# Two linear-attention and squared-ReLU layers on one core: the attention work beside the dense stages written out turn by turn in a fixed engine order, and GpSimd's part of it given to VectorE

## The chip, the core and the metric

The kernel runs on one core of a Trainium2 chip. The engines of that core are named as the profile names them: PE (TensorE, matmuls; PEld is its weight load), DVE (VectorE), ACT (ScalarE), POOL (GpSimd) and SP (SyncE, whose instruction queue here issues the DMA transfers). PSUM is the memory that matmuls write, SBUF the one that all engines read. Each engine works through its own list of instructions in the order of that list; semaphores hold an instruction until its inputs are there. The metric is the device time of one execution in microseconds (us).

## The reference, cut to what matters

Two layers, each an attention block and a dense block with a residual add, on a sequence of S = 2048 rows of D = 576 features, H = 32 heads of 18, and F = 4608 hidden features; the weights of both layers are the same arrays.

```python
def A(x):                                   # x is layernorm(x) of the stream
    q, k, v = split(x @ wqkv)               # 32 heads of 18
    pq, pk  = q @ w_phi, k @ w_phi          # per head
    phi_q = concat(softmax(pq), softmax(-pq))
    phi_k = concat(softmax(pk), softmax(-pk))
    kv, z = phi_k^T v, sum over rows of phi_k      # sums over the whole sequence
    o = (phi_q @ kv) / (phi_q . z + 1e-6)
    return o @ wo
def B(x):
    h = relu(x @ w1 + b1)
    return (h * h) @ w2 + b2
x = x + A(layernorm(x)); x = x + B(layernorm(x))   # twice
```

## The kernel before

**Tiling.** The rows are worked in four blocks of 512 (`TB`), each of four tiles of 128 (`NT`); the hidden features in 36 tiles of 128 (`NF`). Every fp32 operand is held as a high and a low part, and each product is made of three matmuls (high by high, high by low, low by high). Since `kv` and `z` are sums over the whole sequence, a layer's queries can be finished only when the keys of all four blocks are in. So the kernel runs block after block through the dense part (`g_mlp`), and beside the dense part of one block it does the attention work of others: the queries, the output projection and the norm of the block whose dense stage comes next, and, in layer 1, also the norm, keys and values (for layer 2) of the block whose dense stage has just ended.

**A dense stage.** It takes 36 turns, one for a feature tile `f`: `first(f + 1)` brings the weights of the next tile, `hidden(f)` (L703) is 14 matmuls of 512 columns into one PSUM bank called `h`, `square(f)` evacuates that bank on ACT (L709 ReLU with bias, L710 square) and splits the result on DVE (L713 cast to the high part, L714 low part, tile `hb`), and `second(f - 1)` (L729 and L721, 15 matmuls) multiplies the previous tile's result with `w2` into the accumulators `acc`. So `hidden(f + 1)` waits until the ReLU has emptied `h`, and `second(f)` waits for `hb`. In the first dense stage of the whole program the weights are raw fp32: a tile `rr` is loaded (L679, L166, L681; two buffers), copied on ACT into the high part (L682 for `w1`, L684 for `w2`), subtracted on DVE for the low part (L683, L685, and 128 columns of `w2` on POOL at L686), and stored back to DRAM (tile `dw`, L687 and L688). The seven later stages load these parts.

**The attention work.** For each row tile: project (L377) and copy to SBUF (L397); `soft` takes the maximum and minimum of each head (L414, L415), subtracts on DVE (L418, one half of 576 columns) and on POOL (L419, the other half), takes the exponential on ACT (L420) and the sums on DVE (L423). For queries, `g_phi` multiplies with the key sums `zb` (L572 on DVE, L573 on POOL, reduction L574), and scales (L590, one half on each of the two). For keys, POOL does the scaling alone (L431). `g_out` transposes the features (L610), splits them (L611, L612), multiplies with `kv` (L624, L626, L628), projects with `wo` (L646, L649), adds `b2` on POOL (L653), and `g_norm` normalizes and transposes (L321, L335, L336, L337).

**What sets the order.** The attention work is a generator, `g_back`, woven into the turns: one step of it is written behind each turn (a step and a half in layer 1 from the second stage on). That is only the order in which instructions are written; a list scheduler with a cost model then puts each engine's instructions into the order that it deems best, so on ACT and DVE the attention's instructions stand where the scheduler put them. In the stage that follows a bridge, a further rule (`issue_after`) keeps the softmax work behind the last `L714` written.

**The stages of the program**, by the trace (us from the start of the span):

| stage | from | to | dense block | beside it |
|---|---|---|---|---|
| D0 | 266.6 | 543.1 | m_3, raw weights | softmax, output and norm of block 2 |
| D1 | 543.1 | 861.0 | m_2 | norm, values, keys of block 3 for layer 2; queries to norm of block 0 |
| D2 | 861.0 | 1179.3 | m_0 | the same for blocks 2 and 1 |
| D3 | 1179.3 | 1429.0 | m_1 | norm and keys of block 0 for layer 2 |
| bridge | 1429.0 | 1559.3 | none | last keys, sums, queries of two blocks |
| D4 | 1559.3 | 1828.5 | m_1 | softmax, output and norm of the next block |
| D5 | 1828.5 | 2112.2 | m_0 | queries to norm of the next block |
| D6 | 2112.2 | 2395.4 | m_3 | queries to norm of the last block |
| D7 | 2395.4 | 2626.6 | m_2 | nothing |

The names in the trace carry the block (`m_2ph` is the bank `h` of the dense stage of block 2, `a_0Q3e` the exponentials of the fourth query tile of block 0), and the two layers' stages of one block share a name.

## Time and profile before

| | us |
|---|---|
| median of three runs | 2634.07 |
| lowest and highest | 2630.38, 2634.8 |
| the profiled execution: its own time | 2632.79 |
| the profiled execution: span of the trace | 2631.1 |
| granted PE clock, mean over the span | 0.988 |

The span is what the profiler shows of one execution, from the first to the last instruction; 1.7 us of that execution's own time lie around it. The page gives for each engine its busy time and share of the span. A matmul that waits is idle time of PE, and the list of waits gives that idle time by the instruction that ended it. The granted clock tells at which share of full speed PE ran: a busy PE at clock 0.50 does half the work. A row of the timeline reads: start, duration, engine, line, operation, output and inputs, shapes, and in brackets the idle time of that engine before it and what ended it.

### The profile page before, as it was taken

How to read it: one execution, taken by the hardware profiler on the slowest of the kernel's cores; microseconds unless marked ns; L12 is line 12 of the kernel's file. 1: busy time of each engine (PE TensorE's matmuls, PEld its weight loads, DVE VectorE, ACT ScalarE, POOL GpSimd, SP SyncE). 2: the span in 40 equal slices, each digit the busy share in tenths (PEclk: the TensorE clock that was granted, in tenths of full speed). 3: DMA queues.
4: the chain of work that ended last, by engine and by line, in shares of the span. 5: the costliest groups of instructions: out<-in, count | busy, mean ns of one | idle time of the engine just before them, and what ended most of it. 6: DMA issues, size and time to landing. Idle time of an engine off the chain costs nothing.

```text
span 2631.1 us, 37728 instructions
## 1 busy us (share of the span) xinstructions
PE 2548.2 (97%) x15396; PEld 2236.5 (85%) x15396; DVE 1107.3 (42%) x1866; ACT 712.6 (27%) x1180; POOL 380.1 (14%) x425
## 2 busy tenths in 40 slices
PE   8998899999999999999999999999999999999999
PEld 7897688888888888888888987888888888888887
DVE  6777844343623346344212675222622262222111
ACT  3333343422221222313222332212222122212221
POOL 3441411112201022012000222010200030010000
PEclk9998999999999999999999999999999999999999
DMA  8513677885655766556666245556755575556665
GB/s 310 159 55 110 236 261 251 280 299 209 214 169 176 279 209 208 161 202 205 214 198 199 87 154 177 170 181 232 237 181 171 189 235 190 169 182 215 195 199 169
DMA packets 163615, 522.02 MB, mean 198 GB/s; under 512 B 21659, under 2 KB 51003, under 8 KB 161395
## 3 DMA queue, kind: packets, MB, share of 16 engines
q1 hardware_dynamic: 163443, 519.61, 59.7%
q8 instruction: 122, 2.00, 0.3%
q14 instruction: 50, 0.41, 0.0%
HBM read 434.91 MB, written 84.64 MB: 197 GB/s over the span
## 4 chain that ended last, share of the span: by engine, by line
PE 83%; DVE 9%; POOL 2%; DMA 2%; issue 2%; ACT 1%; SPq 0%; DVEq 0%; POOLq 0%; ACTq 0%
PE m_2ph L703 8%; PE m_0ph L703 8%; PE m_1ph L703 8%; PE m_3ph L703 7%; PE m_2acc L729 6%; PE m_1acc L729 6%; PE m_0acc L729 6%; PE m_3acc L729 6%; PE m_2acc L721 2%; PE m_1acc L721 2%; PE m_0acc L721 2%; PE m_3acc L721 2%; PE a_2po L646 1%; PE a_0po L646 1%; PE v_2pv L377 1%
## 5 line engine op out<-in xcount | busy, mean ns | idle before, releaser
L703 PE MATMUL m_0ph<-a_0nh,m_0h 128*128 128x512 f32 (+1 forms) x760 | 230.3, 386 | 7.8 <-ACT m_0hr L709 7.6
L703 PE MATMUL m_2ph<-a_2nh,m_2h 128*128 128x512 f32 (+1 forms) x760 | 228.5, 384 | 3.0 <-ACT m_2hr L709 3.0
L729 PE MATMUL m_3acc<-m_3s,m_3hb 128*128 128x448 f32 x864 | 194.4, 369 | 6.7 <-DVE m_3hb L714 5.1
L729 PE MATMUL m_1acc<-m_1s,m_1hb 128*128 128x448 f32 x864 | 191.9, 369 | 4.7 <-DVE m_1hb L714 2.8
L729 PE MATMUL m_0acc<-m_0s,m_0hb 128*128 128x448 f32 x864 | 190.6, 367 | 1.8 <-DVE m_0hb L713 1.5
L729 PE MATMUL m_2acc<-m_2s,m_2hb 128*128 128x448 f32 x864 | 190.0, 367 | 1.8 <-DVE m_2hb L713 1.5
L729 PEld LDWEIGHTS m_3acc<-m_3s,m_3hb 128*128 128x128 f32 x864 | 161.3, 188 | 28.1 <-DVE m_3hb L714 7.4
L729 PEld LDWEIGHTS m_1acc<-m_1s,m_1hb 128*128 128x128 f32 x864 | 161.9, 189 | 24.8 <-DVE m_1hb L714 4.5
L729 PEld LDWEIGHTS m_2acc<-m_2s,m_2hb 128*128 128x128 f32 x864 | 161.6, 188 | 20.2 <-DVE m_2hb L713 2.0
L729 PEld LDWEIGHTS m_0acc<-m_0s,m_0hb 128*128 128x128 f32 x864 | 161.5, 188 | 20.1 <-DVE m_0hb L713 2.0
L703 PEld LDWEIGHTS m_0ph<-a_0nh,m_0h 128*128 128x128 f32 x760 | 141.2, 190 | 37.6 <-ACT m_0hr L709 8.4
L703 PEld LDWEIGHTS m_2ph<-a_2nh,m_2h 128*128 128x128 f32 x760 | 140.3, 189 | 32.4 <-ACT m_2hr L709 3.4
L713 DVE CAST m_2hb<-m_2hr 128x512 fp32r<-128x512 f32 x72 | 31.7, 440 | 293.1 <-ACT m_2hr L710 293.1
L713 DVE CAST m_1hb<-m_1hr 128x512 fp32r<-128x512 f32 x72 | 32.2, 447 | 268.7 <-ACT m_1hr L710 268.6
L713 DVE CAST m_0hb<-m_0hr 128x512 fp32r<-128x512 f32 x72 | 33.6, 467 | 235.0 <-ACT m_0hr L710 235.0
L709 ACT ACTIVATE m_1hr<-m_1ph,b1t 128x512 f32<-128x512 f32 x72 | 49.4, 686 | 305.5 <-PE m_1ph L703 298.4
L709 ACT ACTIVATE m_2hr<-m_2ph,b1t 128x512 f32<-128x512 f32 x72 | 49.4, 686 | 299.4 <-PE m_2ph L703 285.2
L709 ACT ACTIVATE m_0hr<-m_0ph,b1t 128x512 f32<-128x512 f32 x72 | 49.4, 686 | 273.7 <-PE m_0ph L703 259.5
L703 PE MATMUL m_3ph<-a_3nh,m_3h 128*128 128x512 f32 (+1 forms) x380 | 114.7, 385 | 4.6 <-ACT m_3hr L709 4.6
L703 PE MATMUL m_0ph<-a_0nl,m_0h 128*128 128x512 f32 (+1 forms) x304 | 117.3, 386 | 0.0
L703 PE MATMUL m_3ph<-t0onh,m_3h 128*128 128x512 f32 (+1 forms) x380 | 114.4, 385 | 2.9 <-ACT m_3hr L709 2.5
L703 PE MATMUL m_2ph<-a_2nl,m_2h 128*128 128x512 f32 (+1 forms) x304 | 116.6, 384 | 0.0
(1379 smaller groups left out, 5684.5 us busy)
## 6 DMA issues: line engine op xcount, KB each, us to landing
m_2h<-dw SPq DMA_DIRECT2D x72, 640.0 KB
m_0h<-dw SPq DMA_DIRECT2D x72, 640.0 KB
m_1h<-dw SPq DMA_DIRECT2D x72, 640.0 KB
m_2s<-dw SPq DMA_DIRECT2D x72, 576.0 KB
m_0s<-dw SPq DMA_DIRECT2D x72, 576.0 KB
m_1s<-dw SPq DMA_DIRECT2D x72, 576.0 KB
dw<-m_3h SPq DMA_DIRECT2D x36, 640.0 KB
m_3h<-dw SPq DMA_DIRECT2D x36, 640.0 KB
```

The costliest lines, as they stand in the source:

```text
L377: nc.tensor.matmul(pt[:, :HP], a, m, start=(k == 0), stop=(k == 3 * KC + 1))
L646: nc.tensor.matmul(pt[:, :HP], a, m[:w, g], start=(g == 0 and k == 0), stop=(g == NG - 1 and k == 2))
L703: nc.tensor.matmul(ph[:, cols], a, m, start=(k == 0), stop=(k == 3 * KC + 1))
L709: nc.scalar.activation(hr, ph, AF.Relu, bias=b1t[:, f : f + 1])
L713: nc.vector.tensor_copy(hh, hr)
L721: nc.tensor.matmul(acc[KC], a, m, start=(f == 0 and k == 0), stop=(f == NF - 1 and k == 2))
L729: nc.tensor.matmul(acc[t][:, :R], a[:, rows], m, start=(f == 0 and k == 0), stop=(f == NF - 1 and k == 2))
```

## The change

The change writes the attention work of all eight dense stages as a table of turns, and has PE, ACT, DVE and POOL keep the order in which the instructions are written (`manual_schedule`); SP's transfers, and all that lies outside the dense stages, are still put in order by the scheduler. A turn now has two places where attention work can stand: behind `square(f)`, and behind `second(f - 1)`. `Plan.put(turn, depth, ...)` means the second of them (or, for half turns, the first of the turn after); within a place, deeper (older) work stands first. Each query tile takes three turns: maxima and subtractions in the first, the exponential, the sums and the product with `zb` in the second, the scaling in the third. Everything of the attention that POOL did is now on DVE (L467 for L419, a single 1152-wide multiply L741 for L572 and L573 and L478 for L590 and for L431, L701 for L653, and the whole low part of `w2` at L817); POOL keeps two small operations of each norm. In the dense loop, `first` is cut in two: `first` (the `w1` part) stays ahead of `hidden(f)`, `first2` (the `w2` part) stands behind `second(f - 1)`, and `second(0)` stands behind the first two places of a stage. Attention outputs are transposed and multiplied two a turn instead of one, and the turns of the norm come behind the last projection. The output weights are loaded in the first turns of the queries' work, the query weights and the spilled normalized rows two turns ahead of them. The loop variable `n` is used anew, so that the dense tiles of five stages are called `m3...` in the changed kernel.

```diff
+    class Plan:
+        def put(self, turn, depth, call, *args):
+            slot = round(2 * turn) + 1
+            entries = self.at.setdefault(slot, [])
+            entries.append((-depth, len(entries), call, args))
+        def slots(self):
+            for slot in range(max(self.at, default=-1) + 1):
+                for _, _, call, args in sorted(self.at.get(slot, ()), key=lambda e: e[:2]):
+                    call(*args)
+                yield
...
+    def exponents(raw, name):
...
+        nc.vector.tensor_reduce(mm[:, 0], v, op=ALU.max, axis=AX.X)
+        nc.vector.tensor_reduce(mm[:, 1], v, op=ALU.min, axis=AX.X)
+        nc.vector.tensor_sub(e4[:, 0], v, m[:, 0])
+        nc.vector.tensor_sub(e4[:, 1], m[:, 1], v)
+        return e
+    def totals(e, r):
+        nc.scalar.activation(e, e, AF.Exp)
+        nc.vector.tensor_reduce(r, e.rearrange("p s (h d) -> p s h d", d=DH), op=ALU.add, axis=AX.X)
+        nc.vector.reciprocal(r, r)
+    def scaled(e, r):
...
+        nc.vector.tensor_mul(e3, e3, r2.unsqueeze(2).to_broadcast([P, 2 * H, DH]))
...
-            nc.gpsimd.tensor_add(x, x, b2t)
+            nc.vector.tensor_add(x, x, b2t)
...
+    def plan_queries(plan, at, gap, layer, raws, er, ph, name):
...
+        for t in range(NT):
+            plan.put(at + gap * t, 0, first, t)        # exponents
+            plan.put(at + gap * t + 1, 1, second, t)   # totals, product with zb, its sums
+            plan.put(at + gap * t + 2, 2, third, t)    # scaled
+        return at + gap * (NT - 1) + 2
+    def plan_attend(plan, at, gap, layer, b, raws, dst, name, otags, queries=None):
...
+        if queries:
+            for t in range(NT):
+                plan.put(at + gap * t, 0, queries, t)
+            at += 1
+        for n, call in enumerate(calls):               # loads of the output weights
+            plan.put(at + n, 9, call)
+        at = plan_queries(plan, at, gap, layer, raws, [], out.ph, name) + 1
+        for i in range(2 * NG):
+            plan.put(at + i / 2, 0, out.turn, i)
+            plan.put(at + (i + 1) / 2, 1, out.times, i)
+        at += NG + 1
+        for t in range(NT):
+            plan.put(at + t - 1, 9, out.load, t)
+        plan_norm(plan, Norm(dst, f"{name}n", out.keep), out.project, [at + t for t in range(NT)],
+                  [at + 1, at + 2, at + 4, at + 5], [at + 4 + t for t in range(NT)], [at + 5, at + 7])
...
         def first(f):
...
                 nc.scalar.activation(h1, r1, AF.Copy)
                 nc.vector.tensor_sub(l1, r1, h1.bitcast(F32))
+                nc.sync.dma_start(dense1[f], both1)
...
+        def first2(f):
+            h1, l1, r2, ph = parts[f]
...
             if fresh:
                 nc.scalar.activation(s2[:, :D], r2, AF.Copy)
-                nc.vector.tensor_sub(s2[:, D : D + R], r2[:, :R], s2[:, :R].bitcast(F32))
-                nc.gpsimd.tensor_sub(s2[:, D + R : 2 * D], r2[:, R:], s2[:, R:D].bitcast(F32))
+                nc.vector.tensor_sub(s2[:, D : 2 * D], r2, s2[:, :D].bitcast(F32))
...
         for f in range(2):
             hidden(f, halves[1])
             square(f)
-        second(0)
         yield
         yield
+        second(0)
         first(2)
+        first2(2)
+        yield
+        yield
         for f in range(2, NF):
             if f + 1 < NF:
                 first(f + 1)
             hidden(f, every)
             square(f)
+            yield
             second(f - 1)
+            if f + 1 < NF:
+                first2(f + 1)
             yield
...
+                plan_norm(plan, Norm(xk, f"n{m}"), lambda t, done=done: done[t],
+                          (0, 0, 1, 2), (1, 1, 2, 3), (2, 3, 4, 5), (3, 5))
...
+                    plan.put(4 + t, 0, keys, t)
+                    if i < NB - 1:
+                        plan.put(4 + t, 0, values, t)
+                    plan.put(5 + t, 1, soft1, t)       # exponents of the keys
+                    plan.put(6 + t, 2, soft2, t)       # totals, scaled
+                    if i < NB - 1:
+                        plan.put(7 + t, 3, add, t)
...
+                at = 10
+            if i + 1 < NB:
+                if i == 0:
+                    plan_attend(plan, 0, 3, layer, nb, nxt_raws, nxt, n2, TAGS_C if layer else TAGS_A)
+                else:
...
+                    start = at - 2 if at else 0
+                    for n, call in enumerate(calls):   # loads of the query weights
+                        plan.put(start + n / 4, -2, call)
+                    plan.put(start, -3, lambda held=held, nb=nb, n2=n2: held.update(unspill(nb, f"{n2}u")))
+                    plan_attend(plan, at or 3, 2, layer, nb, raws2, nxt, n2, TAGS_C,
+                                lambda t, held=held, qw=qw, raws2=raws2, n2=n2:
+                                raws2.append(make_raw(held, t, qw, f"{n2}q")))
...
-            weave(g_mlp(layer, b, ready, rows, f"m{n}", layer == 0 and i == 0), g_back(),
-                  1.0 if layer or i == 0 else 1.5)
+            with tc.manual_schedule(engines=ordered):
+                weave(g_mlp(layer, b, ready, rows, f"m{n}", layer == 0 and i == 0), plan.slots(), 1.0)
```

ACT's list in D1, around the last two query tiles of block 0, before the change (`hr` is the dense turn's evacuated tile, `ph` the bank `h`, `a_0Q3e` the exponentials of the last query tile):

```order
L420 ACTIVATE a_0Q2e<-a_0Q2e 128x1152
L709 ACTIVATE m_2hr_7081<-m_2ph_6993,b1t 128x512
L710 ACTIVATE m_2hr_7081<-m_2hr_7081 128x512
L397 ACTIVATE a_0qs_7102<-a_0qp_7103 128x288
L397 ACTIVATE a_0qs_7102<-a_0qp_7119 128x288
L420 ACTIVATE a_0Q3e<-a_0Q3e 128x1152
L709 ACTIVATE m_2hr_7168<-m_2ph_7066,b1t 128x512
L710 ACTIVATE m_2hr_7168<-m_2hr_7168 128x512
```

And the same place in the changed kernel:

```order
L471 ACTIVATE a_0Q2e<-a_0Q2e 128x1152
L420 ACTIVATE a_0qs_7175<-a_0qp_7176 128x288
L420 ACTIVATE a_0qs_7175<-a_0qp_7192 128x288
L837 ACTIVATE m3hr_7225<-m3ph_7130,b1t 128x512
L838 ACTIVATE m3hr_7225<-m3hr_7225 128x512
L837 ACTIVATE m3hr_7276<-m3ph_7210,b1t 128x512
L838 ACTIVATE m3hr_7276<-m3hr_7276 128x512
L471 ACTIVATE a_0Q3e<-a_0Q3e 128x1152
L837 ACTIVATE m3hr_7323<-m3ph_7261,b1t 128x512
L838 ACTIVATE m3hr_7323<-m3hr_7323 128x512
```

Between the copy of the last query tile (L420 now, L397 before) and its exponential there was no other work, so the exponential stood ahead of the next ReLU; now two turns' evacuations stand between them.

DVE's list at the start of D0 before the change (`m_3h_2` and `m_3s_2` are the parts of `w1` and `w2` of tile 2, `hb` the split result, `a_2Q0` the first query tile):

```order
L683 TENSOR_TENSOR m_3h_2_3597<-m_3rr_3599,m_3h_2_3597 128x640
L713 CAST m_3hb_3534<-m_3hr_3531 128x512
L714 TENSOR_TENSOR m_3hb_3534<-m_3hr_3531,m_3hb_3534 128x512
L683 TENSOR_TENSOR m_3h_3_3612<-m_3rr_3614,m_3h_3_3612 128x640
L713 CAST m_3hb_3554<-m_3hr_3551 128x512
L714 TENSOR_TENSOR m_3hb_3554<-m_3hr_3551,m_3hb_3554 128x512
L414 TENSOR_REDUCE a_2Q0m<-t0q2qs_2913 128x32
L415 TENSOR_REDUCE a_2Q0m<-t0q2qs_2913 128x32
L418 TENSOR_TENSOR a_2Q0e<-t0q2qs_2913,a_2Q0m 128x576
```

And in the changed kernel:

```order
L841 CAST m_3hb_3534<-m_3hr_3531 128x512
L842 TENSOR_TENSOR m_3hb_3534<-m_3hr_3531,m_3hb_3534 128x512
L841 CAST m_3hb_3554<-m_3hr_3551 128x512
L842 TENSOR_TENSOR m_3hb_3554<-m_3hr_3551,m_3hb_3554 128x512
L464 TENSOR_REDUCE a_2Q0m<-t0q2qs_2913 128x32
L465 TENSOR_REDUCE a_2Q0m<-t0q2qs_2913 128x32
L466 TENSOR_TENSOR a_2Q0e<-t0q2qs_2913,a_2Q0m 128x576
L467 TENSOR_TENSOR a_2Q0e<-a_2Q0m,t0q2qs_2913 128x576
L804 TENSOR_TENSOR m_3h_2_3583<-m_3rr_3584,m_3h_2_3583 128x640
L817 TENSOR_TENSOR m_3s_2_3593<-m_3rr_3584,m_3s_2_3593 128x576
```

The low part of `w1` of tile 2 (L683, now L804) stood first and now stands behind the four operations of the first query tile.

SP's list in D0 in the changed kernel, where the weights of tile 12 are loaded (`m_3rr_4052` and `m_3rr_4108` are the raw tiles 11 and 12; `dw_11_120` and `dw_11_156` are the stores of the parts of `w1` and `w2` of tile 11; L172 is what L166 was):

```order
L802 DMA m_3rr_4052<-in_B_w 128x576
L800 DMA m_3rr_4108<-in_B_w 128x4x128
L805 DMA dw_11_120<-m_3h_11_4051 128x1280
L172 DMA m_3rr_4108<-in_B_w 64x128
L818 DMA dw_11_156<-m_3s_11_4096 128x1152
L172 DMA m_3rr_4108<-in_B_w 64x128
L802 DMA m_3rr_4108<-in_B_w 128x576
```

One half of the last rows of raw `w1` (the second L172) stands behind the store of tile 11's `w2` part, which is written only behind the previous turn's `second`. In the kernel before, both halves stood ahead of that store, as here at tile 16 (`m_3rr_4401`):

```order
L688 DMA dw_14_159<-m_3s_14_4273 128x1152
L679 DMA m_3rr_4401<-in_B_w 128x4x128
L687 DMA dw_15_124<-m_3h_15_4336 128x1280
L166 DMA m_3rr_4401<-in_B_w 64x128 x2
L681 DMA m_3rr_4401<-in_B_w 128x576
L688 DMA dw_15_160<-m_3s_15_4337 128x1152
```

The raw weights of tile 16 stand behind the store of tile 15's `w1` part alone; the changed kernel has this form in the middle of the stage, and the other for six tiles near its two ends (6, 9, 12, 26, 30, 33).

254 lines of the change are left out of this document (156 added, 98 removed).

## The prediction

> **What bounds the kernel now.** I first asked for the busy time of every engine in each dense stage (columns: stretch, its length, busy time and instructions of PE, PEld, DVE, ACT and POOL, granted clock, share of the DMA engines, GB/s). The rows are D0 to D3, then D4 to D7:
>
> ```profile
> 266.60:543.10 276.50, 266.24 (x1296) 225.55 (x1295) 151.63 (x241) 109.81 (x169) 58.24 (x61) 0.99 0.77 260
> 543.10:861.00 317.90, 312.98 (x1900) 274.34 (x1899) 128.69 (x219) 81.06 (x133) 46.86 (x48) 0.99 0.63 212
> 861.00:1179.30 318.30, 313.13 (x1900) 274.29 (x1899) 129.09 (x221) 80.66 (x132) 46.87 (x48) 0.99 0.63 208
> 1179.30:1429.00 249.70, 248.17 (x1211) 214.64 (x1210) 69.18 (x131) 58.41 (x91) 18.97 (x16) 1.00 0.64 207
> ...
> 1559.30:1828.50 269.20, 264.27 (x1295) 226.30 (x1293) 102.36 (x173) 65.90 (x101) 29.68 (x27) 0.99 0.59 193
> 1828.50:2112.20 283.70, 277.54 (x1400) 240.71 (x1399) 102.04 (x171) 67.09 (x106) 26.87 (x24) 0.99 0.62 204
> 2112.20:2395.40 283.20, 277.32 (x1400) 240.58 (x1399) 102.00 (x170) 67.09 (x106) 26.85 (x24) 0.99 0.58 189
> 2395.40:2626.60 231.20, 230.87 (x1077) 197.65 (x1075) 44.56 (x85) 48.10 (x73) 0.00 (x0) 1.00 0.61 197
> ```
>
> PE is the bound in every stage, and a change that leaves the matmuls as they are can win only PE's idle time. Length less PE busy is 10.26 + 4.92 + 5.17 + 1.53 + 4.93 + 6.16 + 5.88 + 0.33 = 39.2 us. The list of PE's waits (us in total, times, longest) says what ends it:
>
> ```profile
> PE m_0ph L703 <- ACT m_0hr L709: 7.6, 2, 4.6
> PE m_3ph L703 <- ACT m_3hr L709: 7.1, 2, 4.6
> PE m_3acc L729 <- DVE m_3hb L714: 5.1, 5, 1.7
> ...
> PE m_2ph L703 <- ACT m_2hr L709: 3.0, 1, 3.0
> PE m_1acc L729 <- DVE m_1hb L714: 2.8, 2, 2.5
> PE m_1acc L729 <- DVE m_1hb L713: 1.8, 3, 1.2
> PE m_3acc L729 <- DVE m_3hb L713: 1.6, 4, 0.5
> PE m_0acc L729 <- DVE m_0hb L713: 1.5, 2, 1.2
> PE m_2acc L729 <- DVE m_2hb L713: 1.5, 2, 1.2
> PE a_3qp L377 <- DMA a_3uh<-xth: 0.9, 1, 0.9
> ```
>
> The late ReLU costs 7.6 + 7.1 + 3.0 = 17.7 us in five waits; the split result `hb` costs 14.3; the other 7.2 are DMA and the norm's transposes, none above 0.9. The timeline of D1 shows how a ReLU comes late:
>
> ```profile
> 700.34 0.75 DVE L418 TENSOR_TENSOR a_0Q3e<-a_0qs,a_0Q3m 128x576 f32<-128x576 f32 x1
> 700.57 1.54 POOL L419 TENSOR_TENSOR a_0Q3e<-a_0Q3m,a_0qs 128x576 f32<-128x576 f32 x1 [4.87 <-DVE a_0Q3m L415]
> 702.14 1.16 ACT L420 ACTIVATE a_0Q3e<-a_0Q3e 128x1152 f32<-128x1152 f32 x1 [7.10 <-POOL a_0Q3e L419]
> 703.94 0.50 PE L703 MATMUL m_2ph<-a_2nh,m_2h 128*128 128x512 f32 x1 [2.98 <-ACT m_2hr L709]
> ```
>
> ACT has been idle for 7.10 us when the exponential of the last query tile starts: it stands in ACT's list ahead of the ReLU and waits for POOL's half, which waits for DVE. The ReLU comes behind it, and PE stands for 2.98 us. Such a wait costs more than itself, as the same columns show for 3.4 us behind this stall and for an earlier stretch in D0, with the wait in D0:
>
> ```profile
> 328.90:332.30 3.40, 3.14 (x8) 2.68 (x9) 2.21 (x4) 0.65 (x1) 0.00 (x0) 0.52 0.47 193
> 704.50:707.90 3.40, 3.40 (x9) 2.66 (x8) 3.30 (x6) 0.05 (x1) 0.30 (x1) 0.50 0.54 203
> ```
>
> ```profile
> 329.16 1.11 PE L729 MATMUL m_3acc<-m_3s,m_3hb 128*128 128x448 f32 x2 [1.62 <-DVE m_3hb L714]
> ```
>
> The granted clock is half there: PE does 3.4 us' work in 1.7, so 1.7 us are lost. I found six such stretches in the dense stages (the first at 328.9, the last at 2162.1): 6 x 1.7 = 10.2 us. What can be won at all is 39.2 + 10.2 = 49.4 us.
>
> **What a turn takes.** The chain that ended last shows D7, where nothing runs beside:
>
> ```profile
> 2400.61 0.69 ACT m_2hr L709
> ...
> 2401.99 0.44 DVE m_2hb L713
> ...
> 2428.22 2.47 PE m_2acc L729 x12
> 2430.70 0.70 PE m_2acc L721 x3
> 2431.40 3.20 PE m_2ph L703 x14
> ```
>
> A bare turn is 2.47 + 0.70 + 3.20 = 6.4 us. From the start of the ReLU to the end of the cast are 1.8 us, and `hb` is wanted only one `second` and one `hidden` after the bank is full, 6.4 us later: with nothing in the way there are over 3 us of slack on ACT and DVE.
>
> **The change part by part.** *The exponential a turn behind its input* (L471 now in the turn after L467): all five ReLU waits go, 17.7 us.
>
> *POOL's share to DVE.* The prices on DVE and POOL, in the groups of a bridge and in D1:
>
> ```profile
> L586 DVE TENSOR_TENSOR t1fQ0e<-t1fQ0e,t1fr x1: 1357/1357/1357, 1518.9 to 1518.9; 128x1152 f32<-128x1152 f32 x1
> 694.09 1.61 POOL L590 TENSOR_TENSOR a_0Q1e<-a_0Q1e,a_0r 128x576 f32<-128x576 f32 x1
> 694.60 1.72 DVE L590 TENSOR_TENSOR a_0Q0e<-a_0Q0e,a_0r 128x576 f32<-128x576 f32 x1
> ```
>
> A 1152-wide multiply takes DVE 1.36 us, a half of 576 takes 0.75 alone (L418 above), and 1.72 where POOL works beside it. So per query tile DVE gains one subtraction (0.75) and two halves (0.6 each, or nothing where the half was slowed before): 0.75 to 2.0 us; per key tile 0.75 + 1.36 = 2.1; per `b2` add 0.75. In D1 that is at most 4 x (2.0 + 2.1 + 0.75) = 19 us on an engine that is busy 129 of 318. I cost it at nothing, since it lies in the 3 us of slack of a turn that lasts 6.4 us or more; without that cover, 28 query tiles, 12 key tiles and 28 adds come to 56 + 25 + 21 = 102 us, so the cover is what the whole forecast hangs on. The Trainium skill (SBUF — State Buffer, "Who interferes with whom") says that a DVE operation with two SBUF inputs and a POOL operation that reads SBUF exclude each other, the later one blocked until the earlier ends; the trace agrees, since DVE's L590 ended 0.6 us after POOL's 695.70. By that rule DVE's remaining halves get faster once POOL is idle, which speaks against the DVE rival below.
>
> *The order of DVE.* Cast and subtraction of `hb` now stand ahead of the turn's softmax work, so the 14.3 us go but for the starts of stages. `second(0)` still needs `hb(0)` two halves of `hidden` after the ReLU could start; the longest such wait before is 1.2, the shortest 0.3 (m_0acc L713: two, 1.5 together, the longer 1.2). I take 0.5 at seven stages, 3.5 us (2.1 to 8.4).
>
> *Transposes and DMA*, 7.2 us now: the norm's transposes stand two turns behind their input, so of them I leave 1.1 us (0.5 to 2). The transfers get denser: in D1 and D2 the query weights (four tiles of 128x1440 words, 2.9 MB) and the spilled rows (2.4 MB) can be fetched only when the keys' weights are done with, two turns ahead of the first queries, beside 1.2 MB of dense weights a turn. The transfers reached this much:
>
> ```profile
> 885.00:895.00 10.00, 10.00 (x61) 8.89 (x60) 2.23 (x4) 2.16 (x6) 0.00 (x0) 1.00 0.98 371
> ```
>
> Two turns of 8.8 us (317.9 / 36) at 371 GB/s carry 6.5 MB, less 2.4 for the dense weights: 4.1 of the 5.3 MB, so up to 1.2 MB or 3.2 us late. Queries of one tile need only part at once, and the tiles come every second turn, so I take 0.9 in each of D1, D2, D5, D6, 3.5 in all (0 to 12.8).
>
> *D0, where something new is late.* At its start the four operations of query tile 0 (3.0 us at 0.75 each) now stand ahead of the `w1` subtraction of tile 2 (0.8), which `hidden(2)` wants: from the bank's end, `hb` of both tiles is done at about 2.7 (the rows of D7 and one more 0.7), the tile's work at 5.7, the subtraction at 6.5, against 0.5 + 3.2 for `second(0)` plus what of it waits: I take 2.2 us. In four turns 4.1 us of softmax sums (three operations of 1.36) stand between the two weight subtractions; 1.5 + 4.1 + 0.8 + gaps is about 0.4 over a bare turn: 1.6 us. Then the loop of raw weights (load, copy L682, subtract, store `dw`, next load behind it in SP's list). Late in D0 the trace shows it alone:
>
> ```profile
> 493.00 2.05 SPq L166 DMA_DIRECT2D m_3rr<-in_B_w  x2
> 497.72 0.74 ACT L682 ACTIVATE m_3h<-m_3rr 128x640 fp32r<-128x640 f32 x1 [1.68 <-DMA m_3rr<-in_B_w]
> 499.35 0.33 SPq L687 DMA_DIRECT2D dw<-m_3h  x1
> 499.72 1.50 SPq L166 DMA_DIRECT2D m_3rr<-in_B_w  x2
> ```
>
> From issue to issue 6.7 us, 0.3 more than a bare turn; the landing takes 2.7 of it. In the turns behind this one ACT's list before has the ReLU ahead of the copy, so a late copy held nothing; now the copy stands first in every turn, and holds the ReLU. In some 19 turns without attention matmuls that is up to 5.7, and for six tiles half a load waits for the `w2` store besides. I take 4.7. Together D0 keeps 8.5 us (1 to 20).
>
> *Half clock.* The five ReLU stalls and the split's long waits go, and with them the stretches. The Trainium skill (TensorE: Matmul & The Clock Gate, "Part 1: The HAM clock gate") has the rate halved after an idle window of about 3.4 us; by it D0's 2.2 us cost nothing more. The row above has half rate after waits of 1.6 us, so the measurement decides, and I leave 0.8, half a stretch (0 to 3.4).
>
> The sum: kept are 3.5 + 1.1 + 3.5 + 8.5 + 0.8 = 17.4 of 49.4 us, so 32.0 go. The profiled execution (span 2631.1) becomes 2599.1, its own time, 1.7 above the span, 2600.8. The median of the runs before is 1.3 above the profiled one's time: 2602.
>
> With every bound at its low end 3.6 us are kept: 2588. At the high end 46.6: 2631; that all are bad together is unlikely, and half of the overhang gives 2617. The forecast's own range is 2588 to 2618.
>
> **The rivals.** *Transfers crowd.* The 3.2 us come in all four stages, 9.3 more: 2611. For it: share 0.98 in the row above; against: the dense weights are fetched a turn ahead. Chance 0.12.
>
> *DVE becomes the bound of the query turns.* Where a query tile's three parts meet `hb`, the later `hb` costs 0.7 us a tile on 28 tiles, 20 us: 2622. For it: DVE has no reordering left; against: 41% busy in D1. Chance 0.10.
>
> *The ReLU waits move instead of going*, for instance behind copies of keys or transposes on ACT that wait for PE: half of the gain, 16 us: 2618. Chance 0.09. This is also the case that the change does not do what it says.
>
> *Slower: D0's load loop.* With the copy fixed ahead of the ReLU, every bare turn lasts as long as the loop. The gain elsewhere is 32 + 4.7 = 36.7 us; over 19 turns the loop eats it from 1.9 us above 6.4, that is 8.3 us, a landing of 4.3 instead of 2.7. At 4.7 the loop is 8.75: 19 x 2.35 = 45 us, 2602 - 5 + 45 = 2642. For it: D0 has the highest DMA share of all stages, 0.77, and each turn stores 1.2 MB behind which the load queues; against: before, with the same stores, 6.7. Chance 0.08.
>
> **How the numbers follow.** The forecast has 0.61. A difference of 0.2% (5.3 us) is about what a measurement can tell, so faster is below 2628.8. The forecast and the crowded transfers are faster throughout (0.73); of the DVE rival 0.08 and of the moved waits 0.07; of the slower one 0.07 lie above 2639.4. Faster 0.88, same 0.05, slower 0.07. The range takes in the crowded transfers and the DVE rival: 2588 to 2624.
>
> **What would show it.** Right: no wait for a ReLU above 1 us in D1, D2, D5 and D6; no half-clock stretch there; D1 at about 313, D5 and D6 at about 278 us; POOL nearly empty, and DVE near 148 in D1. D0 at about 273 with waits for the `w1` subtraction at its start and copies (now L803) that DMA releases. Wrong: a new wait on `hb` in query turns, DMA waits of several us at the first queries, or D0 longer than 276.5.

## The result

The changed kernel takes 2603.98 us (median of four runs, 2597.93 to 2605.77) against 2632.56 before (four runs, 2630.38 to 2634.8): a ratio of 0.9887, with a 95% interval from 0.9868 to 0.9907. The forecast was 2602, with a range from 2588 to 2624. The profiled execution has 2605.77 us, the longest of the four, and a span of 2604.1, 27.0 below the span before.

The busy times by stage after the change, D0 to D3 and D4 to D7, with the columns of the table in the prediction:

```profile
265.80:535.10 269.30, 263.89 (x1293) 226.41 (x1292) 159.46 (x260) 109.47 (x169) 6.26 (x10) 0.99 0.79 266
535.10:851.40 316.30, 312.30 (x1900) 275.00 (x1900) 142.19 (x243) 81.02 (x133) 6.81 (x24) 0.99 0.65 219
851.40:1164.90 313.50, 310.55 (x1899) 273.96 (x1898) 142.47 (x244) 80.59 (x132) 7.50 (x32) 1.00 0.62 211
1164.90:1415.10 250.20, 248.59 (x1210) 214.70 (x1210) 77.16 (x135) 58.65 (x91) 3.23 (x8) 1.00 0.62 200
...
1544.50:1808.00 263.50, 261.49 (x1294) 225.59 (x1292) 109.35 (x192) 64.78 (x101) 3.95 (x10) 1.00 0.64 207
1808.00:2088.40 280.40, 277.29 (x1400) 241.09 (x1400) 106.99 (x186) 66.51 (x106) 3.15 (x8) 0.99 0.63 205
2088.40:2366.30 277.90, 275.78 (x1400) 239.91 (x1399) 106.87 (x186) 66.52 (x106) 3.15 (x8) 1.00 0.56 185
...
sum 2202.70, PE 2181.10 PEld 1894.33 DVE 887.98 ACT 575.63 POOL 34.07; mean PE 272.64 PEld 236.79 DVE 111.00 ACT 71.95 POOL 4.26
```

The sum row gives the eight stages together: 2202.7 us, of which PE is busy 2181.1, so 21.6 us of PE's idle time are left of 39.2. D0 gave 7, D4 and D6 between 5 and 6, D2 nearly 5, D5 3, D1 1.6; D3 and D7 gave nothing. What PE still waits for in the changed kernel (us in total, times, longest):

```profile
PE m3ph L831 <- DMA m3h<-dw: 8.4, 6, 2.8
...
PE m_3ph L831 <- DVE m_3h L804: 2.1, 3, 1.6
PE m_3ph L831 <- ACT m_3hr L837: 1.9, 1, 1.9
PE m3acc L857 <- DVE m3hb L841: 1.5, 5, 0.3
PE k_2kp L400 <- DVE n_2l L353: 1.2, 1, 1.2
PE k_0kp L400 <- DVE n_0l L353: 1.2, 1, 1.2
PE k_3kp L400 <- DVE n_3l L353: 1.2, 1, 1.2
PE t0onp L351 <- DVE t0onn L336: 1.0, 1, 1.0
```

Of 17.7 us behind late ReLUs one wait of 1.9 is left, in D0; the 14.3 us behind `hb` have become waits of 0.3 at the starts of stages. The largest is new: 8.4 us for the parts of `w1` (1.2 us of such waits before). So are three waits of 1.2, in which the projection of a key tile stands behind the low part of the norm.

### The profile page after: what moved, and what is told of

Read it like the earlier page. It is cut to its first block, busy times and chain, and to the rows that moved or that the text cites. A ratio compares the mean times of both kernels' runs of the same rounds, so it can differ in the third digit from the quotient of the medians.

```text
span 2604.1 us, 37449 instructions
## 1 busy us (share of the span) xinstructions
PE 2538.0 (97%) x15396; PEld 2235.8 (86%) x15396; DVE 1170.4 (45%) x1994; ACT 710.1 (27%) x1180; POOL 148.5 (6%) x261
## 4 chain that ended last, share of the span: by engine, by line
PE 89%; DVE 4%; DMA 2%; POOL 1%; issue 1%; ACT 1%; SPq 0%; DVEq 0%; POOLq 0%; ACTq 0%
PE m3ph L831 22%; PE m3acc L857 16%; PE m3acc L849 5%; PE m_2ph L831 4%; PE m_1ph L831 4%; PE m_3ph L831 4%; PE m_2acc L857 3%; PE m_1acc L857 3%; PE m_3acc L857 3%; DMA m3h<-dw 2%; PE a_2po L694 1%; PE a_0po L694 1%; PE m_2acc L849 1%; PE m_1acc L849 1%; PE k_3kp L400 1%
## 5 line engine op out<-in xcount | busy, mean ns | idle before, releaser
L857 PE MATMUL m3acc<-m3s,m3hb 128*128 128x448 f32 x2160 | 474.9, 368 | 1.8 <-DVE m3hb L841 1.5
L857 PEld LDWEIGHTS m3acc<-m3s,m3hb 128*128 128x128 f32 x2160 | 403.4, 188 | 46.6 <-DVE m3hb L841 2.5
L837 ACT ACTIVATE m3hr<-m3ph,b1t 128x512 f32<-128x512 f32 x180 | 123.7, 687 | 788.9 <-PE m3ph L831 788.9
L831 PE MATMUL m3ph<-a_0nh,m3h 128*128 128x512 f32 (+1 forms) x760 | 228.9, 386 | 4.2 <-DMA m3h<-dw 4.2
L831 PEld LDWEIGHTS m3ph<-a_0nh,m3h 128*128 128x128 f32 x760 | 140.5, 189 | 32.5 <-issue 4.7
L849 PE MATMUL m3acc<-m3hb,m3s 128*128 128x512 f32 x540 | 153.9, 395 | 0.0
L842 DVE TENSOR_TENSOR m3hb<-m3hr,m3hb 128x512 fp32r<-128x512 f32 x180 | 124.6, 692 | 6.2
L831 PE MATMUL m3ph<-a_2nh,m3h 128*128 128x512 f32 (+1 forms) x380 | 115.1, 388 | 2.5 <-DMA m3h<-dw 2.5
L831 PE MATMUL m3ph<-a_0nl,m3h 128*128 128x512 f32 (+1 forms) x304 | 116.5, 383 | 0.0
L831 PE MATMUL m_2ph<-a_2nh,m_2h 128*128 128x512 f32 (+1 forms) x380 | 112.8, 381 | 0.0
L841 DVE CAST m_2hb<-m_2hr 128x512 fp32r<-128x512 f32 x36 | 15.4, 427 | 183.9 <-ACT m_2hr L838 183.9
```

Source lines behind the costliest of these rows:

```text
L831: nc.tensor.matmul(ph[:, cols], a, m, start=(k == 0), stop=(k == 3 * KC + 1))
L837: nc.scalar.activation(hr, ph, AF.Relu, bias=b1t[:, f : f + 1])
L841: nc.vector.tensor_copy(hh, hr)
L842: nc.vector.tensor_sub(hl, hr, hh.bitcast(F32))
L849: nc.tensor.matmul(acc[KC], a, m, start=(f == 0 and k == 0), stop=(f == NF - 1 and k == 2))
L857: nc.tensor.matmul(acc[t][:, :R], a[:, rows], m, start=(f == 0 and k == 0), stop=(f == NF - 1 and k == 2))
```

## The experiments

Each run below was compared with the kernel before on the same chip; ratios are to that. "Dense sum" is the length of the eight dense stages in the profiled execution: 2229.7 us before, 2202.7 after.

### 1. Order and share, one at a time

With the order of the changed kernel, and POOL's share given back (the scaling, the `b2` add and 128 columns of the low part of `w2` likewise):

```diff
-        nc.vector.tensor_sub(e4[:, 1], m[:, 1], v)
+        nc.gpsimd.tensor_sub(e4[:, 1], m[:, 1], v)
...
-            nc.vector.tensor_mul(m, e, zb)
+            nc.vector.tensor_mul(m[:, 0], e[:, 0], zb[:, 0])
+            nc.gpsimd.tensor_mul(m[:, 1], e[:, 1], zb[:, 1])
...
+            for s in range(2):
+                e3 = e[:, s].rearrange("p (h d) -> p h d", d=DH)
+                (nc.gpsimd if s else nc.vector).tensor_mul(e3, e3, r[:, s].unsqueeze(2).to_broadcast([P, H, DH]))
...
-            nc.vector.tensor_add(x, x, b2t)
+            nc.gpsimd.tensor_add(x, x, b2t)
```

> The changed kernel's turns and fixed order, but GpSimd gets its whole former share back (one half of the softmax subtraction, the key scaling, half of the query product and of the scaling, the b2 add, 128 columns of the w2 low part). Theory A (the order makes the gain; the share is hidden either way): 2600 to 2612 us, no wait for the ReLU above 1 us in D1, D2, D5, D6. Theory B (GpSimd's slow halves and its slowing of VectorE make the waits): at least half of the 28 us comes back, 2618 to 2632 us, with waits on hb in the query turns.

With the order that the scheduler made before, and the share on DVE everywhere:

> The kernel before with its scheduler's order, only GpSimd's share given to VectorE. Theory A (order): the scheduler still puts the last exponential close ahead of a ReLU, so most waits stay: 2622 to 2640 us. Theory B (share): the exponential's input is there 0.8 us after the first half instead of 1.5, VectorE is no longer slowed, and most of the gain shows: 2604 to 2618 us.

The same, with the share moved in the dense stages alone, which is the scope of the change:

```diff
+    beside = {"g": nc.gpsimd}
...
-        nc.gpsimd.tensor_sub(e4[:, 1], m[:, 1], v)
+        beside["g"].tensor_sub(e4[:, 1], m[:, 1], v)
...
             rows = []
+            beside["g"] = nc.vector
             weave(g_mlp(layer, b, ready, rows, f"m{n}", layer == 0 and i == 0), g_back(),
...
+            beside["g"] = nc.gpsimd
```

> The kernel before with its scheduler's order; GpSimd's share goes to VectorE in the dense stages alone, as in the change, and stays with GpSimd in the part ahead of them and in the bridges. Theory C (either edit cures the same waits: the share alone takes about 34 us out of the dense stages, the rest of the 48 us of the run with the share alone came from the front and the bridges, 11 and 5 us): 2594 to 2604 us, dense stages together 2193 to 2201 us against 2230.6 before and 2203.7 in the changed kernel. Rival (the share gains mainly through the front, or only with it): above 2610 us.

| | order by the scheduler | order fixed, by turns |
|---|---|---|
| POOL has its share | 2632.6, dense sum 2229.7 | 2607.3, dense sum 2203.1 |
| share on DVE in the dense stages | 2598.3, dense sum 2197.0 | 2604.0, dense sum 2202.7 |
| share on DVE everywhere | 2583.6, dense sum 2195.3 | 2585.2, dense sum 2195.8 (experiment 4) |

The sum rows of the kernel before, of the order alone and of the share alone in the dense stages:

```profile
sum 2229.70, PE 2190.51 PEld 1894.07 DVE 829.55 ACT 578.12 POOL 254.34; mean PE 273.81 PEld 236.76 DVE 103.69 ACT 72.26 POOL 31.79
```

```profile
sum 2203.10, PE 2179.79 PEld 1891.96 DVE 813.51 ACT 574.44 POOL 258.25; mean PE 272.47 PEld 236.49 DVE 101.69 ACT 71.81 POOL 32.28
```

```profile
sum 2197.00, PE 2180.36 PEld 1889.03 DVE 874.95 ACT 578.58 POOL 35.66; mean PE 272.54 PEld 236.13 DVE 109.37 ACT 72.32 POOL 4.46
```

PE's idle time (length less busy) is 39.2 us before, 23.3 with the order alone and 16.6 with the share alone, against 21.6 with both. The ratios are 0.9906 (0.9887 to 0.9926) for the order alone, 0.9870 (0.9856 to 0.9885) for the share alone in the dense stages, 0.9818 (0.9801 to 0.9835) for the share everywhere (D0 then starts at 255.5 instead of 266.6, and the bridge is 5.1 us shorter, so 16 of its 49 us lie outside the dense stages), and 0.9887 (0.9868 to 0.9907) for both edits of the change. So theory A was right that the order alone brings the gain, and wrong that the share alone does not (2583.6 lies below both ranges expected of that run, 2598.3 within theory C's): either edit takes out nearly all of the same waits, and the two together take out no more than one. With the order alone 4.7 us of waits for the ReLU are left, all in D0, 4.1 of them behind a copy of raw weights that comes late (experiment 5). The share alone in the dense stages is not slower than both: 2598.3 to 2604.0, with intervals that overlap; and with the share everywhere, the fixed order adds nothing that can be told (2583.6 and 2585.2). The share is not a single cause, though: with it the scheduler also made another order on DVE and ACT, and these runs do not separate that order from POOL's slower halves.

How the ReLU is freed with the share alone shows in the timeline of D1, in the run with the share on DVE in the dense stages (DVE's rows first, then ACT's):

```profile
690.16 0.75 DVE L420 TENSOR_TENSOR a_0Q3e<-a_0Q3m,a_0qs 128x576 f32<-128x576 f32 x1
690.83 1.35 DVE L587 TENSOR_TENSOR a_0Q0e<-a_0Q0e,a_0r 128x1152 f32<-128x1152 f32 x1
```

```profile
690.94 0.69 ACT L709 ACTIVATE m_2hr<-m_2ph,b1t 128x512 f32<-128x512 f32 x1 [2.81 <-PE m_2ph L703]
691.52 1.16 ACT L421 ACTIVATE a_0Q3e<-a_0Q3e 128x1152 f32<-128x1152 f32 x1
```

In this run the scheduler puts the last tile's subtractions ahead of the scaling of the first tile, and the ReLU ahead of the exponential; neither waits for the other. Before, DVE's list had the older tiles' work first (here in D5, with ACT's rows below):

```profile
1871.64 0.74 DVE L572 TENSOR_TENSOR a_3m<-a_3Q2e,zb 128x576 f32<-128x576 f32 x1
1872.48 1.35 DVE L574 TENSOR_REDUCE a_3u<-a_3m 128x64 f32<-128x1152 f32 x1
1873.75 0.74 DVE L414 TENSOR_REDUCE a_3Q3m<-a_3qs 128x32 f32<-128x576 f32 x1
...
1875.07 0.75 DVE L418 TENSOR_TENSOR a_3Q3e<-a_3qs,a_3Q3m 128x576 f32<-128x576 f32 x1
```

```profile
1867.77 0.41 ACT L397 ACTIVATE a_3qs<-a_3qp 128x288 f32<-128x288 f32 x1 [1.45 <-PE a_3qp L377]
1876.88 1.16 ACT L420 ACTIVATE a_3Q3e<-a_3Q3e 128x1152 f32<-128x1152 f32 x1 [8.70 <-POOL a_3Q3e L419]
```

The raw values of the last query tile were copied by 1868.2, and DVE came to them at 1873.75, so the exponential, next in ACT's list, was late by more than the slack of the ReLU behind it.

### 2. Is it the turn between subtraction and exponential?

```diff
     def totals(e, r):
-        nc.scalar.activation(e, e, AF.Exp)
...
             er.append(exponents(raws[t], f"{name}Q{t}"))
+            nc.scalar.activation(er[t], er[t], AF.Exp)
...
                         es[t] = exponents(ks.pop(t), f"k{m}K{t}")
+                        nc.scalar.activation(es[t], es[t], AF.Exp)
```

> The changed kernel with each exponential written right behind its subtractions, in the same turn, so that it stands one turn earlier in ScalarE's list. By the prediction's step (the turn between subtraction and exponential removes the ReLU waits) the waits of 3 to 4.6 us come back: 2620 to 2632 us. By the rival (what counts is that hb stands ahead of the softmax work on VectorE and that both halves are VectorE's; the exponential is then late by less than the 3 us of slack that the ReLU has): 2600 to 2608 us, no wait for the ReLU above 0.5 us.

Measured: 2628.7 us, ratio 0.9986 (0.9975 to 0.9997), as the prediction's step had it by the number, but not by the mechanism. PE's waits in that run:

```profile
PE v_2pv L400 <- ACT k_2ks L420: 8.0, 3, 4.1
PE m3ph L831 <- DMA m3h<-dw: 7.4, 6, 2.0
PE v_3pv L400 <- ACT k_3ks L420: 6.2, 3, 3.2
...
PE m3ph L831 <- ACT m3hr L837: 0.9, 1, 0.9
```

The waits for the ReLU are 0.9 us in one place, in D3, and 0.8 in D0; the 14.2 us are another wait, in the keys' turns of D1 and D2. D1 and D2 together are 21.2 us longer than in the changed kernel, of which these waits, and four half-clock stretches against one, make up 19.3. And this is the work of the keys in D1 and of the queries in D5, on ACT:

```profile
609.32 1.16 ACT L1017 ACTIVATE k_3K1e<-k_3K1e 128x1152 f32<-128x1152 f32 x1 [7.12 <-DVE k_3K1e L467]
610.38 0.69 ACT L420 ACTIVATE k_3ks<-k_3kp 128x288 f32<-128x288 f32 x2
```

```profile
1883.21 0.69 ACT L837 ACTIVATE m3hr<-m3ph,b1t 128x512 f32<-128x512 f32 x1 [2.81 <-PE m3ph L831]
...
1890.84 1.17 ACT L734 ACTIVATE a_3Q1e<-a_3Q1e 128x1152 f32<-128x1152 f32 x1 [6.28 <-DVE a_3Q1e L467]
1891.91 0.67 ACT L837 ACTIVATE m3hr<-m3ph,b1t 128x512 f32<-128x512 f32 x1
```

For the queries the exponential stands ahead of a ReLU again and waits 6.28 us for DVE; the ReLU follows at 1891.91, and PE does not wait. But this is not the place that it had before: the subtractions are written a turn behind the projection, so one evacuation, the ReLU at 1883.21, stands between the copy of the raw values (done at 1880.4) and the exponential, where before there was none. In the changed kernel there are two; its DVE and ACT at the last query tile of D1, whose raw values were copied by 697.8 and whose first ReLU behind that was at 700.59:

```profile
704.16 1.36 DVE L478 TENSOR_TENSOR a_0Q2e<-a_0Q2e,a_0r 128x1152 f32<-128x1152 f32 x1
...
707.43 0.75 DVE L467 TENSOR_TENSOR a_0Q3e<-a_0Q3m,a_0qs 128x576 f32<-128x576 f32 x1
```

```profile
706.88 0.69 ACT L837 ACTIVATE m3hr<-m3ph,b1t 128x512 f32<-128x512 f32 x1 [4.95 <-PE m3ph L831]
...
708.21 1.17 ACT L471 ACTIVATE a_0Q3e<-a_0Q3e 128x1152 f32<-128x1152 f32 x1
```

From the copy to the end of the subtractions it takes 10.4 us here and in the run above, more than the 8.7 before, and the last tile's subtractions still stand behind the scaling of an older tile. So the fixed order does not make the exponential's input earlier; it lets the ReLUs pass ahead of the exponential. In the run above D5 takes 277.4 us and D6 277.7, not more than in the changed kernel. For the keys the exponential stands ahead of the copies that empty the next tile's projection out of PSUM, and the projection of the values stands until a bank is free. So the turn between subtraction and exponential is needed for the keys, where several banks change hands in a turn, and not for the queries, where it was credited with the gain: there one evacuation between copy and exponential was enough.

### 3. The table of turns without the fixed order

```diff
-            with tc.manual_schedule(engines=ordered):
+            with nullcontext():
```

> The changed kernel's written turns and share, but the scheduler orders all engines. Theory A1 (the table of turns is enough, the scheduler keeps near to it): 2600 to 2610 us. Theory A2 (the order must be fixed, since the scheduler pulls the exponentials up to the ReLU again): 2615 to 2635 us, with waits for the ReLU of 1 to 4 us at the last query tiles.

Measured: 2612.4 us, ratio 0.9927 (0.9906 to 0.9947): between the two expectations, and for a reason that neither had.

```profile
PE t0opt L653 <- DVE t0fQ2e L632: 10.5, 1, 10.5
PE t1opt L653 <- DVE t1fQ2e L632: 10.4, 1, 10.4
PE m3acc L857 <- DVE m3hb L841: 8.3, 5, 2.6
...
PE m3ph L831 <- DMA m3h<-dw: 0.7, 2, 0.5
```

The dense sum is 2194.3, shorter than with the fixed order. But the scheduler pulls the softmax work of D0 and D4 forward into the stretches ahead of them, in front of the scaling that the transposes there wait for: 10.5 and 10.4 us, against 6.6 and 3.7 at the same two places in the changed kernel. D0 starts at 275.4 instead of 265.8. The dense sum is shorter in part because that work now lies outside it. The six stages whose work is the same (D1 to D3, D5 to D7) take 1664.0 us against 1669.9, and the ReLU waits do not come back. Inside the stages the fixed order is thus no better than the scheduler's with the same table; what it does is keep the stages' work out of the bridges, and `hb` ahead (8.3 us of waits here).

### 4. What is left, and where else POOL's share lies

With POOL's share on DVE also ahead of the dense stages and in the bridges:

```diff
-        nc.gpsimd.tensor_sub(e4[:, 1], m[:, 1], v)
+        nc.vector.tensor_sub(e4[:, 1], m[:, 1], v)
...
-        nc.gpsimd.tensor_mul(e3, e3, r2.unsqueeze(2).to_broadcast([P, 2 * H, DH]))
+        nc.vector.tensor_mul(e3, e3, r2.unsqueeze(2).to_broadcast([P, 2 * H, DH]))
```

> The changed kernel, with GpSimd's softmax share given to VectorE also ahead of the dense stages and in the bridges. If the front and the bridges have 16 us of their own to give: 2584 to 2594 us, the first dense stage starts at about 255 instead of 266. If that gain needs the scheduler's freedom inside the stages: 2598 to 2606 us.

Measured: 2585.2 us, ratio 0.9822 (0.9807 to 0.9837), 18.8 below the changed kernel. D0 starts 6.3 us earlier (259.5), the bridge is 5.2 shorter (129.4 to 124.2), and the dense sum is 6.9 lower. The last is in places that this edit does not touch, and the changed kernel's own four runs lie 7.8 us apart, so of the 18.8 some 11 are the edit's by its places. The time lies in the expected range, but front and bridge gave these 11 us and not 16.

Moves against the remaining waits: query weights and rows get three turns, the queries' work starts a turn later, and the norm's transposes stand behind the keys' projection of their turn (`deep` is -1 there and 2 elsewhere). The third turn is new in D1 and D2 alone; in D5 and D6 the changed kernel had three already, and there everything comes a turn later:

```diff
-                    start = at - 2 if at else 0
+                    start = 8 if at else 1
                     for n, call in enumerate(calls):
-                        plan.put(start + n / 4, -2, call)
+                        plan.put(start + n / 2, -2, call)
...
-                    plan_attend(plan, at or 3, 2,
+                    plan_attend(plan, 11 if at else 4, 2,
...
-            plan.put(turns[t], 2, norm.turn, t)
+            plan.put(turns[t], deep, norm.turn, t)
```

> The changed kernel with three small moves against its remaining waits: the query weights and spilled rows get three turns instead of two ahead of the first queries and come one piece a half turn instead of a quarter, the queries' work starts one turn later, and the norm's transposes stand behind the keys' projection of their turn. If the 8.4 us of waits for dense weights and the 3.6 us of key projections behind the norm's low part are what they look like, with the two half-clock stretches behind them: 2587 to 2596 us, no DMA wait above 1 us in D1, D2, D5, D6. Rival (the transfers only shift, since the amount is the bound): 2600 to 2606 us.

Measured: 2594.0 us, ratio 0.9852 (0.9838 to 0.9867), dense sum 2190.1. The three waits for the norm are gone, and D1 is down from 316.3 to 312.1 us; the DMA waits fall only to 4.7, and not all below 1 us as expected:

```profile
PE m3ph L831 <- DMA m3h<-dw: 4.7, 6, 2.5
```

Of these, 3.5 us stand at the starts of D5 and D6, where the moved loads no longer are. Both sets of moves together:

> The last two together. If their gains lie in different places they add: 2569 to 2584 us, below the 2583.6 of the share alone under the scheduler. If not: 2584 to 2592 us.

Measured: 2580.4 us, ratio 0.9804 (0.9787 to 0.9820), 23.6 below the changed kernel; the two gains (18.8 and 10.0) add for the most part. To try whether the starts of D5 and D6 wait because the first tile's weights are freed late, the first two tiles ran at full width:

```diff
-            hidden(f, halves[0])
-        for f in range(2):
-            hidden(f, halves[1])
-            square(f)
+            hidden(f, halves[0] if split else every)
+            if not split:
+                square(f)
+        for f in range(2 if split else 0):
+            hidden(f, halves[1])
+            square(f)
```

> The last kernel (share on VectorE everywhere, loads spread), and in the six stages that do not follow a bridge the first two tiles of hidden run over all 512 columns at once instead of half by half, so that the first tile's weights are free and its result is squared 1.6 us earlier. If the waits of 1.4 to 2.3 us for the weights of tile 2 at the start of D5 and D6, and the 0.3 us for hb at each start, come from that late release: 2573 to 2579 us, DMA waits at those starts below 1 us. If the transfers at the stage's start are bound by their amount: 2578 to 2582 us.

Measured: 2585.8 us (2582.9 to 2588.3), ratio 0.9816 (0.9799 to 0.9833): no gain, longer than either expectation, and the waits grew.

```profile
PE m3ph L831 <- DMA m3h<-dw: 10.7, 7, 4.6
```

SP issued the load of tile 2's `w1` part 3.9 and 3.7 us behind the first store of finished rows in D5 and D6, against 4.8 in both before this edit, so the earlier release moved the issue by about 1 us only; and in D5 PE had the weights 10.0 us after that issue, against 8.0. So an earlier release of the buffer does not bring the weights earlier. What makes the transfers late at these starts is not settled; the four stores of finished rows and a load of `w2` parts, which SP issues just ahead of this load, were not tried.

### 5. The loop of raw weights in D0

The prediction had a load stand behind a store of the previous tile in SP's list, and the copy hold the ReLU. In the changed kernel it happened at tile 9 (SP's rows: the store of tile 8's `w2` part, then half a load; ACT's copy; PE):

```profile
320.65 0.33 SPq L818 DMA_DIRECT2D dw<-m_3s  x1
321.02 0.47 SPq L172 DMA_DIRECT2D m_3rr<-in_B_w  x1
```

```profile
326.02 0.74 ACT L803 ACTIVATE m_3h<-m_3rr 128x640 fp32r<-128x640 f32 x1 [5.13 <-issue]
326.66 0.67 ACT L837 ACTIVATE m_3hr<-m_3ph,b1t 128x512 f32<-128x512 f32 x1
```

```profile
327.38 0.50 PE L831 MATMUL m_3ph<-t0onh,m_3h 128*128 128x512 f32 x1 [1.94 <-ACT m_3hr L837]
```

The copy has waited for 5.13 us and the ReLU stands behind it. For this wait the page names no releaser ("issue"); that it is the half load is read from SP's list. In the run with the order alone, where half a load stands behind the store in the same way, the page names it:

```profile
330.34 0.74 ACT L809 ACTIVATE m_3h<-m_3rr 128x640 fp32r<-128x640 f32 x1 [5.48 <-DMA m_3rr<-in_B_w]
```

PE's wait behind that one is 2.34 us. With the stores issued by POOL's queue, which has little else to do there (POOL is busy 6.3 us of D0):

```diff
-                nc.sync.dma_start(dense1[f], both1)
+                nc.gpsimd.dma_start(dense1[f], both1)
...
-                nc.sync.dma_start(dense2[f], both2)
+                nc.gpsimd.dma_start(dense2[f], both2)
```

> The changed kernel with one edit: D0's stores of the split weights go by GpSimd's queue. By the prediction's step on D0 (a load of raw w1 stands in SP's list behind a store that waits for the previous tile's w2 part, the copy is late and holds the ReLU): the ReLU wait of 1.9 us at tile 9 and the half-clock stretch behind it go, D0 266 us instead of 269.5, median 2598 to 2603. Rival (the copies wait for the transfers' amount): D0 269 to 271 us and 2602 to 2607.

Measured: 2596.7 us (2595.1 to 2601.7), just below the expected 2598, ratio 0.9864 (0.9850 to 0.9878). What ACT's copies of raw `w1` waited for, in the changed kernel and then in this run (us, times):

```profile
  DMA m_3rr<-in_B_w: 39.2, 17
```

```profile
  DMA m_3rr<-in_B_w: 16.2, 10
```

The wait for the ReLU in D0 is down from 1.9 to 0.6 us in two pieces, there is no half-clock stretch in D0, and D0 takes 266.9 us against 269.3. So the load does wait behind the store, and the rival (the transfers' amount) is out as the cause of most of the copies' waits: the amount is the same. What the wait costs is less clear. The runs of experiment 4 leave D0 as it is in the changed kernel and have the copies wait 35.6 to 39.9 us too, yet D0 takes 267.0 to 267.9 us in them, so that most of the 2.4 us is the spread from one execution to the next; the three runs with the stores on POOL's queue have 265.7, 266.9 and 267.1. That is 1 us or so. Of the 7.3 us between the medians, whose intervals overlap, at most these 2.4 lie in D0; the rest are places that the edit leaves alone. On top of full-width starts and of the run with both sets of moves:

> The same, and in D0 the stores of the split weights are issued by GpSimd's queue instead of SyncE's, so that no load of raw weights stands behind a store. By the prediction's step (the loop of raw weights: a load waits in SP's list for a store, the copy stands ahead of the ReLU): the wait for the ReLU in D0 (1.0 to 2.0 us and a half-clock stretch) goes, copies wait less for DMA than the 39 us in the changed kernel, D0 shorter by 1 to 4 us. Rival (the copies wait for the transfers' own time): D0 unchanged within 1 us, or longer because GpSimd's queue is slower.

> The run with both sets of moves (2580.4 us), with half-wide starts, and D0's stores on GpSimd's queue. If the store loop costs D0 what it seemed to (1.3 us between the last two runs' D0, up to 3.6 with its half-clock stretch): 2575 to 2580 us, no ReLU wait in D0.

Measured: 2579.6 us, ratio 0.9796 (0.9778 to 0.9814), with D0 1.3 us shorter than in the run with full-width starts and no ReLU wait in it; and 2578.5 us, ratio 0.9786 (0.9773 to 0.9800), where D0 was hardly shorter (267.4 to 267.0) and one ReLU wait of 1.0 stayed, against the expectation. The last is the fastest median of the study, 25.4 us below the changed kernel; it can't be told from the two runs at 2579.6 and 2580.4, whose ranges it overlaps.

## Why the prediction was right, and where it was not

The time was right (2602 forecast, 2604.0 measured), and so were the bound (PE, to be won by its waits), the removal of the ReLU and `hb` waits, and the share's cost of nothing within the fixed order: 2607.3 with POOL, 2604.0 without, although DVE's busy time in D1 goes from 127 to 142 us between these two. That it came so close is partly luck. By the prediction's own count 26.7 us are kept (21.6 idle, 5.1 at half clock), not 17.4; some 4 us that it did not count came back; and the profiled execution, 27.0 us shorter where 32.0 were forecast, is 1.8 above the median, where the forecast took it to be 1.3 below. Term by term:

- *What can be won* was counted as 49.4 us. PE's idle time fell by 17.6 and its busy time in the dense stages from 2190.5 to 2181.1, 9.4 us, of which three fewer half-clock stretches explain 5.1. So some 4 us lay inside PE's busy time that the count left out; what they are is not shown.
- *ReLU waits*: all five go; right by size. The reason given, a turn between subtraction and exponential, is what failed: without that turn the ReLU waits did not come back (experiment 2), and the scheduler's own order without POOL had none above 0.2 us either (experiment 1). What the cures have in common is only that no ReLU stands behind an exponential that is later than the ReLU's slack. The fixed order gets there by evacuations that stand between the copy and the exponential; the scheduler with the share on DVE by doing the last tile's subtractions at once, 2.8 us from copy to end.
- *`hb` at the starts of stages*: 3.5 forecast, 2.3 by the list of waits. (Of the waits before, the 14.3 leave out two of 0.3 us; with them it is 14.9, and the rest 6.6 instead of 7.2.) *Transposes*: 1.1 forecast, 1.9 for the two at bridges; but 3.6 us came where the step saw none: the keys' projection behind the norm's low part of the same turn, which a change of their order inside the turn removed.
- *DMA*: 3.5 forecast, 9.2 measured (8.4, and 0.8 in D4), inside its bounds of 0 to 12.8. It shows as dense weights that come late, not as queries that wait. In D1 and D2 (2.5 and 1.4 us at the queries' loads) the step was right, since more time for the loads took it to 0.5 and 0.3; at the starts of D5 and D6 the loads of queries were not the cause.
- *D0*: 8.5 us kept by forecast, of them 2.2 for tile 2 at the start (1.6 measured), 1.6 in the softmax turns (0.5), 4.7 for the load loop (1.9 of wait and a half-clock stretch of 1.7 behind it). The mechanism held, with one stall where six were possible.
- *Half clock*: 0.8 forecast, with a bound of 3.4; three stretches measured, 5.1 us (each is 3.4 us in which PE does the work of 1.7; the prediction's words have it the other way round). They lie in D0, D1 and D5, where for D1 and D5 the prediction named their absence as a sign of being right; the last two windows here begin some 0.6 us late and 0.2 us early, so their mean clock is above 0.50:

```profile
328.00:331.40 3.40, 3.40 (x10) 2.62 (x9) 3.20 (x8) 1.19 (x2) 0.00 (x0) 0.50 0.70 280
635.80:639.20 3.40, 3.40 (x10) 2.63 (x10) 1.28 (x1) 0.00 (x0) 0.00 (x0) 0.59 1.00 405
1822.80:1826.20 3.40, 3.40 (x10) 2.60 (x9) 0.00 (x0) 0.00 (x0) 0.00 (x0) 0.53 0.67 265
```

They follow waits of 1.94, 2.17 and 2.75 us, while the 1.6 us at D0's start had none behind it, nor had one of 2.54 in D0 before the change. The Trainium skill (TensorE: Matmul & The Clock Gate, "Part 1: The HAM clock gate") asks for an idle window of about 3.4 us; none of these three waits was so long, and the clock was halved. The choice of 0.8, half a stretch, was too low.

The rivals: crowded transfers came in part (5.7 us over the forecast); the DVE rival, the moved ReLU waits and the slower one did not come. The signs of being wrong came in part as well: waits for DMA of several us, though not at the first queries, and D1 at 316.3 instead of 313. The case that was not among the rivals is that one half of the change alone would do as much as the whole.

## What to carry to other kernels

When a change makes two edits at once, build each alone before crediting the gain to either: here each of them removed nearly the same waits, and the simpler one, moving the slow engine's share, was enough under this scheduler. A fixed order is worth most where it keeps work of one stage out of another's critical stretch; what it cost here is that a copy whose load is late holds what stands behind it (the copies of raw weights waited 15.4 us for their loads before and 39.2 after), so look next at each load that stands behind a store. Once a trace has shown a half-clock stretch behind a short PE wait, price such waits with a chance of one: here waits of 1.9 to 2.8 us had it, and one of 2.54 did not. And before crediting a gain to a single stage, look at how far that stage differs between runs in which it is the same: here up to 2.3 us.

## What the runs showed that was not expected

POOL's queue carried D0's stores of 1.2 MB a turn without any cost that shows: its issues took 0.53 us each, and DVE, PE and the loads were not slower for it. With the weights' buffer released earlier at the starts of six stages, the waits for weights were longer (10.7 us in all against 4.6), which is left open.
